# Where the left rows' layernorm sums are made and taken: two softmax stages, and a copy on ScalarE

## The chip, the cores and the metric

The kernel runs on one core of a Trainium2 chip. The metric is the device time of one execution in microseconds; of the kernel before there are three runs, and their median counts.

## The reference, cut to what matters

Rows are normalised (layernorm) and go through an attention layer that walks over 64 segments of 32 rows. Each segment puts 8 memory rows ahead of its 32 rows, attends over the 40, and hands on its first 8 output rows as memory to the next segment, so segments follow one another strictly. A small router part works on two chosen rows and is added at the end.

```
xn = layernorm(x)
for s in range(64):                       # segments of 32 rows
    h = concat([mem, xn[32*s:32*s+32]])   # 8 + 32 rows
    q, k, v = h @ Wq, h @ Wk, h @ Wv      # 32 heads of 128
    p = softmax(mask(q @ k.T * scale))
    o = (p @ v) @ Wo
    mem, out_s = o[:8], o[8:]
out = x + concat(out_s) + expert_of_two_rows(xn)
```

## The kernel before, in words

**Weights.** They are cut into 64 granules of 512 KB (48 for q, k and v, 16 for Wo). 44 stay in the SBUF; 20 are streamed again in each segment through 5 slots (`g`), one of them kept in PSUM instead. SP issues the fetches (L407); a fetch waits until TensorE has used up the granule that was in its slot.

**Order of a segment.** TensorE walks through phases 0 to 5 (q, k for heads 0 to 15, then q, k for heads 16 to 31, then v of both halves) with 8 granules each (`kc` 0 to 7), 4 matmuls a granule (L886), and then through the 16 granules of Wo (`w` 0 to 15, L615 and L619). Everything else hangs on these places by a table of hooks: `hook(p, kc, fn)` runs `fn` behind the matmuls of that granule, and hooks of one place run in the order in which they are entered. Since each engine works through its queue in order, the place of a hook is the place of its instructions in every queue that it uses.

**Attention in the hooks.** Each half of the heads goes through: transposes of q and k into the PSUM tile BT (L690), with copies out on ScalarE or VectorE (L698, L703, L705); scores into the PSUM tile BS (L713, L715) with mask and maximum on VectorE (L722 to L728); the exponent on ScalarE (L732); the rest of the softmax on VectorE (`soften`, L737 to L761); and `attend` on TensorE (L778, L780) with copies on ScalarE (L789, L791). The first half's scores are at (2,6), its exponent and softmax at (3,4), its `attend` at (5,4) and (5,6); the second half's transposes of k are at (4,3), its scores at (4,6), its exponent and softmax at (5,0), and its `attend` at w 5 and w 8. ScalarE copies the rows to be transposed (XB, L905) and the values (VM, L915) at each phase's end.

**Left rows.** A segment's last 8 rows ("left" rows) are not worked on in their own segment: those of four segments are gathered, 32 at a time, and go through the matmuls as extra passes over granules in the group before (L606, L639). Four segments make a group; the first segment of a group (`j == 0`) loads the next group's left rows and takes their layernorm statistics. That happens in the segments 4, 8, ..., 56; the preamble and segment 0 do it at once, by `stats_now`.

**Statistics.** `part_stats` (L206, L207) and `split_stats` (L210, L212, L213) are five small VectorE instructions in the tile SW; a row's elements lie in four groups of partitions, so `sum_stats` adds them up by small matmuls into BT's last columns (L216 for one order of rows, four times L219 for the other), and `take_sums` (L223) adds two halves and brings the sums back to SW, on VectorE. For the left rows `take_left` does that twice. In segments 4 to 56 these stood at (2,7), (4,0) and (4,1). `spread_of` (L227, L229) and `root_of` (L232, L233) make the factor of it, later. The next segment's own rows use the same S6, AV and HL columns of SW at (5,0).

BT carries the sums in columns 504 to 511, and the transposes and half of `attend` in others; what writes BT waits for those that read it before.

Of the kernel before, what the change touches and what calls it, by code (L numbers as in the profile page):

```python
# [51 lines left out]
def kernel(  # L52
# [16 lines left out]
    nc = tc.nc  # L69
# [9 lines left out]
    NT = S // P  # L79
# [79 lines left out]
    BT = psT.tile([P, 512], F32, name="BT")  # L159
# [6 lines left out]
    SW = const.tile([P, 24], F32, name="SW")  # L166
    S6, AV, HL, AB = SW[:, 0:6], SW[:, 6:8], SW[:, 0:2].bitcast(BF16), SW[:, 14:16]
    ROWS = [SW[:, 10:14], SW[:, 16:20]]
    NEGR, KMSK = SW[:, 20:21], SW[:, 21:22]
    OUTER = [SW[:, 8:10], SW[:, 22:24]]  # L170
    SPREAD, ROOT = SW[:, 2:3], SW[:, 3:4]
    SUMS = BT[:, 508:512]
    SUMS2 = BT[:, 504:508]
# [31 lines left out]
    def part_stats(x):  # L205
        nc.vector.bn_stats(out=S6, in_=x)  # L206
        nc.vector.bn_aggr(out=AV, in_=S6)  # L207

    def split_stats():
        nc.vector.scalar_tensor_tensor(out=AV[:, 1:2], in0=AV[:, 0:1], scalar=AV[:, 0:1], in1=AV[:, 1:2],  # L210
                                       op0=ALU.mult, op1=ALU.add)
        nc.vector.tensor_scalar(out=HL[:, 0:2], in0=AV, scalar1=0.25, scalar2=None, op0=ALU.mult)  # L212
        nc.vector.scalar_tensor_tensor(out=HL[:, 2:4], in0=AV, scalar=0.25, in1=HL[:, 0:2], op0=ALU.mult, op1=ALU.subtract)  # L213

    def sum_stats(crossed=False):
        nc.tensor.matmul(SUMS, lhsT=S4, rhs=HL, start=True, stop=True, skip_group_check=True)  # L216
        if crossed:
            for h in range(0, P, 32):
                nc.tensor.matmul(SUMS2[h:h + 32, :], lhsT=S1, rhs=HL, start=True, stop=True, tile_position=(0, h),  # L219
                                 skip_group_check=True)  # L220

    def take_sums(r, sums=SUMS):
        nc.vector.tensor_reduce(out=r[:, 0:2], in_=sums.rearrange("p (h c) -> p c h", h=2), axis=AX.X, op=ALU.add)  # L223

    def spread_of(r, to=None):
        to = r[:, 2:3] if to is None else to
        nc.vector.scalar_tensor_tensor(out=to, in0=r[:, 0:1], scalar=r[:, 0:1], in1=r[:, 1:2],  # L227
                                       op0=ALU.mult, op1=ALU.subtract)
        nc.vector.tensor_scalar(out=to, in0=to, scalar1=0.0, scalar2=1e-5, op0=ALU.min, op1=ALU.subtract)  # L229

    def root(of, to):
        nc.scalar.activation(out=to, in_=of, func=ACTF.Ln, scale=-1.0)  # L232
        nc.scalar.activation(out=to, in_=to, func=ACTF.Exp, scale=-0.5)  # L233

    def root_of(r):
        root(r[:, 2:3], r[:, 3:4])

    def take_left(G):
        take_sums(ROWS[1])
        take_sums(OUTER[G % 2], SUMS2)  # L240

    def stats_now(x, G=None):
        part_stats(x)
        split_stats()
        sum_stats(G is not None)
        if G is None:
            take_sums(ROWS[0])
        else:
            take_left(G)
        r = ROWS[G is not None]  # L250
        spread_of(r)
        root_of(r)
# [238 lines left out]
    todo_res = [g for g in resident if g not in res_tiles]  # L491

    stats_now(X[0][:, :])
    xn = norm_seg(0)
    stats_now(XL0, 0)
    norm_left(XL0)
    ST, STL = new_st(turn_rows(xn, XL0))
# [175 lines left out]
    for s in range(NSEG):  # L673
        G, j = divmod(s, 4)
# [6 lines left out]
        QT, KT, PTs, OT, nxt, sums = {}, {}, {}, {}, {}, {}  # L681
        hooks = {}

        def hook(p, kc, fn):
            hooks.setdefault((p, kc), []).append(fn)
# [21 lines left out]
        def scores(half):  # L707
            QKL = qkl[0]
            q, k = QT[half], KT[half]
            for il in range(4):  # L710
                for jq in range(4):
                    hh = 4 * il + jq
                    nc.tensor.matmul(SPS[32 * jq:32 * jq + 32, il, 0, :], lhsT=q[:, hh, :], rhs=k[:, hh, :],  # L713
                                     start=(il == 0), stop=True, tile_position=(0, 32 * jq), skip_group_check=True)
                    nc.tensor.matmul(SPS[32 * jq:32 * jq + XL, il, 1, :], lhsT=QKL[:, il, 2 * half, jq, :],  # L715
                                     rhs=k[:, hh, :], start=False, stop=True, tile_position=(0, 32 * jq),
                                     skip_group_check=True)
            for S4, m in ((SPS[:, :, 0, 0:XM], MASK), (SPS[:, :, 0, SEG:NK], None),
                          (SPS[:, :, 1, SEG:NK], MASK[:, 0:XL])):
                if m is not None:  # L720
                    m = m.unsqueeze(1).to_broadcast([P, 4, S4.shape[2]])
                    nc.vector.tensor_tensor(out=S4, in0=S4, in1=m, op=ALU.add)  # L722
                else:
                    nc.vector.tensor_scalar(out=S4, in0=S4, scalar1=NEGR, scalar2=None, op0=ALU.add)
            S8 = SPS.rearrange("p i a k -> p (i a) k")
            NM = one.tile([P, 8], F32, tag="nm", name="NM")
            nc.vector.tensor_reduce(out=NM[:, :], in_=S8, axis=AX.X, op=ALU.max, negate=True)
            nc.vector.tensor_tensor(out=S8, in0=S8, in1=NM[:, :].unsqueeze(2).to_broadcast([P, 8, NK]), op=ALU.add)  # L728
# [119 lines left out]
        if j == 0 and G + 1 < NT:  # L848
            hook(*((4, 1) if s == 0 else (1, 0)), get_left)
            if s > 0:  # L850
                hook(2, 7, lambda: part_stats(nxt["xl"]))
                hook(2, 7, split_stats)
                hook(4, 0, lambda: sum_stats(True))
                hook(4, 1, lambda: take_left(G + 1))
                hook(5, 7, lambda: spread_of(ROWS[1]))
            else:
                hook(5, 7, lambda: stats_now(nxt["xl"], G + 1))
# [5 lines left out]
            hook(2, 4, lambda: load_seg(s + 1))  # L863
        hook(4, 6, lambda: scores(1))
        hook(5, 0, exponent)
        if s + 1 < NSEG:
            hook(*((5, 0) if j == 0 else (4, 5)), lambda: part_stats(X[(s + 1) % 2][:, :]))
            hook(5, 0, split_stats)
        else:
            hook(1, 0, router_out)  # L870
            hook(1, 6, router_in)
# [232 lines left out]
```

## Time and profile before

| | |
|---|---|
| three runs | 1911.12, 1911.48, 1911.91 us |
| the profiled execution | 1903.86 us, its span 1902.2 us |
| mean TensorE clock | 0.954 |
| busy: PE, DVE, ACT, POOL | 84%, 52%, 41%, 24% of the span |
| TensorE idle at L690 until L223 | 30.5 us, 14 times |
| TensorE idle at L886 until a streamed granule | 59.8 us, 116 times |

The profile is of one execution. A timeline row gives the start, the busy time, the engine, the line, the operation with what it writes and reads, and in brackets how long the engine sat idle before it and who ended that. A row of waits gives the engine and line that waited, for whom, the total, how many times, and the longest. A window's row gives the busy time of each engine in it, then TensorE's granted clock (1.00 is full), the DMA engines' busy share and GB/s.

### The profile page before, as it was taken

To read this page: it belongs to the slowest core of one execution; us is meant where nothing else is said; L and a number is where in the kernel's file an instruction comes from. 1 tells how busy PE (TensorE), PEld (TensorE's weight loads), DVE (VectorE), ACT (ScalarE), POOL (GpSimd) and SP (SyncE) were. 2 spreads that over 40 slices of the span, in tenths; PEclk is the share of its full clock that TensorE was granted. 3 is DMA by queue.
4 is the path that set the end of the run, shared out by engine and by line. 5 is a ranking of instruction groups with operands and counts; after the bars stand their busy time and mean duration, and the time that the engine had idled before them with its cause. 6 is when DMAs were issued, how large, how long until landed. Compare 5 with 4: busy or idle time off the path is not lost.

```text
span 1902.2 us, 78103 instructions
## 1 busy us (share of the span) xinstructions
PE 1605.4 (84%) x33352; PEld 804.9 (42%) x33352; DVE 985.7 (52%) x3261; ACT 774.8 (41%) x2443; POOL 455.3 (24%) x895
## 2 busy tenths in 40 slices
PE   4478888988889989898888889898988989889864
PEld 2134444444444444444444444444444444444333
DVE  2135555555556555654565555556555555555540
ACT  1024444444444444444443444444444444444330
POOL 2212313222131313213131322323132221312120
PEclk9579999999999999999999999999999999999995
DMA  9999999999999999999999999999999999999998
GB/s 367 390 346 385 364 376 368 374 380 358 380 364 395 360 375 382 364 379 334 392 356 371 377 357 380 362 399 356 396 377 370 388 361 386 354 379 384 371 377 345
DMA packets 228061, 707.66 MB, mean 372 GB/s; under 512 B 38913, under 2 KB 52833, under 8 KB 227713
## 3 DMA queue, kind: packets, MB, share of 16 engines
q1 hardware_dynamic: 190272, 666.72, 92.4%
q0 software_dynamic: 28640, 28.03, 4.6%
q10 hardware_dynamic: 8800, 7.92, 1.2%
q8 instruction: 261, 4.28, 0.9%
q14 instruction: 88, 0.71, 0.1%
HBM read 689.86 MB, written 22.29 MB: 374 GB/s over the span
## 4 chain that ended last, share of the span: by engine, by line
DMA 56%; PE 37%; DVE 3%; ACT 2%; issue 1%; SPq 0%; POOL 0%; ACTq 0%; DVEq 0%; POOLq 0%
DMA g<-wsc 47%; PE PSm L886 21%; PE PSl L606 5%; PE BT L690 3%; PE WO L619 2%; PE WL L639 2%; DMA wres<-in_A_Wk_dram 2%; DMA wres<-in_A_Wv_dram 1%; DMA g<-in_A_Wo_dram 1%; DMA g<-in_A_Wv_dram 1%; DMA MW<-in_B_w_gate_dram 1%; DMA MW<-in_B_w_up_dram 1%; PE WO L615 1%; DMA X<-in_A_x_dram 1%; PE WO L778 1%
## 5 line engine op out<-in xcount | busy, mean ns | idle before, releaser
L886 PE MATMUL PSm<-wres,ST 128*32 128x512 bf16 x8448 | 709.3, 389 | 27.0 <-DMA wres<-in_A_Wv_dram 14.5
L886 PEld LDWEIGHTS <-ST 128*32 128x32 bf16 x12288 | 317.9, 97 | 390.8 <-issue 161.4
L886 PE MATMUL PSm<-g,ST 128*32 128x512 bf16 x3588 | 365.4, 393 | 70.7 <-DMA g<-wsc 59.8
L905 ACT CAST XB<-PSm 128x512 bf16<-128x512 f32 x256 | 150.6, 588 | 254.2 <-PE PSm L886 251.5
L522 POOL DMA_DIRECT2D LX<-ql_d x63 | 35.6, 564 | 653.1 <-PE WO L619 264.4
L705 DVE COPY KT<-BT 128x512 bf16<-128x512 bf16 x112 | 46.1, 411 | 280.7 <-PE BT L690 280.6
L972 POOL DMA_DIRECT2D out_dram<-X x256 | 129.4, 512 | 241.5 <-DVE X L970 219.5
L606 PE MATMUL PSl<-wres,STL 128*32 128x512 bf16 x2112 | 185.6, 392 | 0.2 <-ACT XBl L910 0.2
L318 POOL DMA_DIRECT2D X<-in_A_x_dram x252 | 127.3, 511 | 190.9 <-PE PSm L886 122.3
L430 ACT COPY BK<-KEPT 128x512 bf16<-128x512 bf16 x189 | 111.7, 605 | 136.9 <-DMA ql_d<-XBl 66.6
L619 PEld LDWEIGHTS <-OT 128*32 128x32 bf16 x4096 | 100.1, 96 | 107.2 <-issue 79.6
L619 PE MATMUL WO<-g,OT 128*32 128x256 bf16 x1536 | 78.0, 279 | 69.0 <-DMA g<-wsc 56.2
L690 PE MATMUL BT<-IDENT,XB 128*128 128x128 bf16 x1024 | 102.8, 224 | 32.2 <-DVE SW L223 30.5
L698 ACT COPY QT<-BT 128x512 bf16<-128x512 bf16 x128 | 74.9, 585 | 122.3 <-PE BT L529 73.5
L615 PE MATMUL WO<-wres,OT 128*32 128x512 bf16 x1536 | 122.2, 383 | 0.0
L690 PEld LDWEIGHTS <-XB 128*128 128x128 bf16 x1024 | 60.1, 98 | 139.4 <-ACT XB L905 69.1
L619 PE MATMUL WO<-wres,OT 128*32 128x256 bf16 x2560 | 115.4, 276 | 0.3 <-issue 0.3
L722 DVE TENSOR_TENSOR BS<-BS,CT 128x96 f32<-128x96 f32 (+1 forms) x256 | 59.4, 232 | 108.5 <-PE BS L715 103.7
L778 PEld LDWEIGHTS <-VM 32*128 32x128 bf16 x2048 | 65.3, 91 | 115.2 <-issue 88.6
L915 ACT CAST VM<-PSm 128x512 bf16<-128x512 f32 x128 | 75.9, 593 | 76.0 <-PE PSm L886 75.8
L606 PEld LDWEIGHTS <-STL 128*32 128x32 bf16 x3072 | 83.6, 98 | 50.1 <-issue 6.6
L703 ACT COPY KT<-QKL 128x128 bf16<-128x128 bf16 x128 | 38.1, 298 | 152.4 <-PE BT L690 152.4
(191 smaller groups left out, 2756.1 us busy)
## 6 DMA issues: line engine op xcount, KB each, us to landing
g<-wsc SPq DMA_DIRECT2D x1134, 512.0 KB, 6.2
g<-wsc SPq DMA_DIRECT2D x63, 256.0 KB, 5.7
LX<-ql_d POOLq DMA_DIRECT2D x63, 128.0 KB, 5.7
ql_d<-XBl ACTq DMA_DIRECT2D x60, 128.0 KB, 5.7
MW<-in_B_w_gate_dram SPq DMA_DIRECT2D x16, 448.0 KB, 9.5
MW<-in_B_w_up_dram SPq DMA_DIRECT2D x16, 448.0 KB, 9.0
wres<-in_A_Wk_dram SPq DMA_DIRECT2D x12, 512.0 KB, 15.9
wres<-in_A_Wq_dram SPq DMA_DIRECT2D x11, 512.0 KB, 5.3
```

What stands on the lines that cost most here:

```text
L318: by.dma_start(out=X[s % 2][32 * g:32 * g + XM, :], in_=x2[s * SEG:s * SEG + XM, 256 * block(g):256 * (block(g) + 1)])
L430: copy(out=back[c][:, :], in_=KEPT_COLS[KEPT_WHOLE][c])
L606: nc.tensor.matmul(PSl[32 * jq:32 * jq + 32, :], lhsT=STL[:, g % KC, :], rhs=part(Gv, jq), start=first_, stop=last_, tile_position=(0, 32 ...
L615: nc.tensor.matmul(PS[r0:r0 + 32, :], lhsT=lhs(h), rhs=Gv[:, D * hs + 512 * c:D * hs + 512 * (c + 1)], start=(w == 0), stop=(w == N_WIDE - ...
L619: nc.tensor.matmul(PS[32 * g:32 * g + 32, 0:256], lhsT=lhs(h), rhs=Gv[:, D * hs + 256 * block(g):D * hs + 256 * (block(g) + 1)], start=(w ...
L690: nc.tensor.transpose(out=PTq[:, il, :, :].rearrange("p j r -> p (j r)"), in_=XB[:, il * P:(il + 1) * P], identity=IDENT[:, :])
L698: nc.scalar.copy(out=QT[half][:, :, :], in_=pv)
L778: nc.tensor.matmul(o, lhsT=VM[half][q0:q0 + 32, il * P:(il + 1) * P], rhs=PTm[q0:q0 + 32, il, 0:NK], start=True, stop=False, tile_position ...
L886: nc.tensor.matmul(PSm[32 * jq:32 * jq + 32, :], lhsT=ST[:, 2 * block(kc // 2) + kc % 2, :], rhs=part(Gv, jq), start=(kc == 0), stop=(kc = ...
L905: nc.scalar.copy(out=XB[:, :], in_=PSm[:, :])
L915: nc.scalar.copy(out=VM[half][:, :], in_=PSm[:, :])
L972: nc.gpsimd.dma_start(out=out2[s * SEG:s * SEG + XM, 256 * block(g):256 * (block(g) + 1)], in_=OB[32 * g:32 * g + XM, :])
```

## The change

In segments 4, 8, ..., 56 the five statistics instructions of the left rows move from (2,7), behind the first half's scores, to (4,0), behind the first softmax. Their sums move from (4,0) to (4,7), behind the second half's scores. The sums are no longer taken out of BT by VectorE at (4,1): ScalarE copies all 8 columns to SW at (4,7) (`hold_left`), and VectorE adds the halves from there at (5,0), ahead of the next segment's statistics. `stats_now`, for the preamble and segment 0, gets the same copy.

```diff
+    def hold_left():
+        nc.scalar.copy(out=SW[:, 0:8], in_=BT[:, 504:512])
+
     def take_left(G):
-        take_sums(ROWS[1])
-        take_sums(OUTER[G % 2], SUMS2)
+        take_sums(ROWS[1], SW[:, 4:8])
+        take_sums(OUTER[G % 2], SW[:, 0:4])
...
         else:
+            hold_left()
             take_left(G)
...
             if s > 0:
-                hook(2, 7, lambda: part_stats(nxt["xl"]))
-                hook(2, 7, split_stats)
-                hook(4, 0, lambda: sum_stats(True))
-                hook(4, 1, lambda: take_left(G + 1))
+                hook(4, 0, lambda: part_stats(nxt["xl"]))
+                hook(4, 0, split_stats)
+                hook(4, 7, lambda: sum_stats(True))
+                hook(4, 7, hold_left)
...
         hook(5, 0, exponent)
+        if j == 0 and 0 < s and G + 1 < NT:
+            hook(5, 0, lambda: take_left(G + 1))
```

On VectorE, in segment 4, from the statistics of the left rows (BX) to the second half's scores (L722); L660 belongs to the left rows' output, L737 to L761 are the first softmax. Before:

```order
L206 BN_STATS SW<-BX 128x6
L207 BN_AGGR SW<-SW 128x2
L210 SCALAR_TENSOR_TENSOR SW<-SW 128x1
L212 TENSOR_SCALAR SW<-SW 128x2
L213 SCALAR_TENSOR_TENSOR SW<-SW 128x2
L660 TENSOR_TENSOR LF<-WL,LF 64x256 x2
L737 TENSOR_REDUCE DN<-BS 128x8
L738 RECIPROCAL DN<-DN 128x8
```

The softmax's other rows follow here, and behind its last (L761) stand the two L223 and then L722. After the change (lines are 4 higher there from `take_left` on) the same stretch ends so:

```order
L765 STREAM_TRANSPOSE PT_3655<-BX 128x256
L206 BN_STATS SW<-BX 128x6
L207 BN_AGGR SW<-SW 128x2
L210 SCALAR_TENSOR_TENSOR SW<-SW 128x1
L212 TENSOR_SCALAR SW<-SW 128x2
L213 SCALAR_TENSOR_TENSOR SW<-SW 128x2
L726 TENSOR_TENSOR BS<-BS,CT 128x4x24
L728 TENSOR_SCALAR BS<-BS,SW 128x4x8
L726 TENSOR_TENSOR BS<-BS,CT 128x4x8
L731 TENSOR_REDUCE NM<-BS 128x8
L732 TENSOR_TENSOR BS<-BS,NM 128x320
L223 TENSOR_REDUCE SW<-SW 128x2 x2
```

The five instructions moved from ahead of L660 and the softmax to behind it, and the two reductions from ahead of the second scores' five steps to behind them; they now read SW.

On TensorE, in segment 4 at (4,3), the last matmul of the granule and the first of the transposes into BT, with what each waits for. Before:

```order
L886 LDWEIGHTS ST
L886 MATMUL PSm<-wres_603,ST 32x512
L690 LDWEIGHTS XB [waits Activation_49]
L690 MATMUL BT<-IDENT,XB 128x128 [waits DVE_49]
L690 LDWEIGHTS XB
```

After:

```order
L892 LDWEIGHTS ST
L892 MATMUL PSm<-wres_604,ST 32x512
L694 LDWEIGHTS XB [waits Activation_49]
L694 MATMUL BT<-IDENT,XB 128x128
L694 LDWEIGHTS XB
```

The transposes no longer wait for VectorE; they still wait for ScalarE's copy of the rows.

On TensorE at (4,7), between the last granule of phase 4 (`g`) and the first of phase 5 (`wres_724`, in the changed kernel `wres_725`). Before:

```order
L886 LDWEIGHTS ST
L886 MATMUL PSm<-g,ST 32x512
L886 LDWEIGHTS ST
L886 MATMUL PSm<-wres_724,ST 32x512 [waits PE_49]
L886 LDWEIGHTS ST
```

After:

```order
L892 LDWEIGHTS ST
L892 MATMUL PSm<-g,ST 32x512
L216 LDWEIGHTS S_142
L216 MATMUL BT<-SW,S_142 128x4 [waits DVE_49]
L219 LDWEIGHTS S_147
L219 MATMUL BT<-SW,S_147 32x4
```

Three more pairs of L219 and then the granule `wres_725` follow. The sums, with their wait for VectorE's L213, now stand ahead of all of phase 5.

## The prediction

> **What bounds the kernel now.** First the page, for the span and for who is busy, then the same busy shares cut by segment: segment 4 (the first of a group, the only kind that the change touches) and segment 5 behind it.
>
> ```profile
> span 1902.2 us, 78103 instructions
> q1 hardware_dynamic: 190272, 666.72, 92.4%
> DMA 56%; PE 37%; DVE 3%; ACT 2%; issue 1%; SPq 0%; POOL 0%; ACTq 0%; DVEq 0%; POOLq 0%
> 204.80:233.20 28.40, 24.42 (x503) 12.10 (x496) 17.09 (x62) 13.03 (x43) 10.34 (x20) 0.94 0.97 352
> 233.20:260.10 26.90, 23.89 (x515) 12.11 (x511) 14.49 (x47) 11.55 (x36) 4.91 (x11) 1.00 1.02 389
> ```
>
> The last two rows give start:end, length, busy time of PE, PEld, DVE, ACT and POOL, then TensorE's clock, DMA share and GB/s. Weights stream all the time; where the slots are full, the stream waits for TensorE, and where they are empty TensorE waits for it. Segment 4 is 1.5 us longer than segment 5 although TensorE has no more instructions in it (503 against 515), and the stream moves 352 GB/s in it instead of 389. So something stops TensorE there, and the stream with it. The list of waits names it:
>
> ```profile
> PE PSm L886 <- DMA g<-wsc: 59.8, 116, 1.7
> PE BT L690 <- DVE SW L223: 30.5, 14, 2.5
> PE BT L216 <- DVE SW L213: 19.3, 16, 10.6
> ```
>
> The middle row has 14 waits, one in each first segment of a group from 4 to 56: 30.5 / 14 = 2.18 us each. In segment 4, TensorE's timeline and then VectorE's (start, us, what, and in brackets the idle time before it):
>
> ```profile
> 216.04 0.18 PE L216 MATMUL BT<-SW,S 128*128 128x4 bf16 x1 [0.36 <-DVE SW L213]
> 216.19 0.39 PE L886 MATMUL PSm<-g,ST 128*32 128x512 bf16 x4
> 219.17 0.38 PE L690 MATMUL BT<-IDENT,XB 128*128 128x128 bf16 x4 [2.16 <-DVE SW L223]
> 220.48 0.23 PE L713 MATMUL BS<-KT,QT 128*32 128x40 bf16 x4 [0.17 <-ACT KT L705]
> 221.12 1.10 PE L886 MATMUL PSm<-wres,ST 128*32 128x512 bf16 x8
> 223.44 0.21 PE L778 MATMUL WO<-PT,VM 32*128 32x40 bf16 x1
> 226.59 0.19 PE L778 MATMUL BS<-PT,VM 32*128 32x40 bf16 x1
> 231.38 0.40 PE L619 MATMUL WO<-g,OT 128*32 128x256 bf16 x8 [0.97 <-DMA g<-wsc]
> ```
> ```profile
> 214.70 0.42 DVE L206 BATCH_NORM_STATS2 SW<-BX 128x6 f32<-128x256 bf16 x1
> 215.82 0.16 DVE L213 SCALAR_TENSOR_TENSOR SW<-SW 128x2 bf16<-128x2 f32 x1
> 215.96 0.86 DVE L660 TENSOR_TENSOR LF<-WL,LF 64x256 f32<-64x256 f32 x2
> 217.96 0.29 DVE L756 TENSOR_TENSOR BX<-BS,DN 128x64 bf16<-128x64 f32 x1
> 218.56 0.45 DVE L761 STREAM_TRANSPOSE PT<-BX 128x256 bf16<-128x256 bf16 x1
> 218.93 0.19 DVE L223 TENSOR_REDUCE SW<-BT 128x2 f32<-128x4 f32 x2
> 221.00 0.27 DVE L722 TENSOR_TENSOR BS<-BS,CT 128x96 f32<-128x96 f32 x1 [1.89 <-PE BS L715]
> 225.67 0.45 DVE L761 STREAM_TRANSPOSE PT<-BX 128x256 bf16<-128x256 bf16 x1
> 226.04 0.12 DVE L223 TENSOR_REDUCE SW<-BT 128x2 f32<-128x4 f32 x1
> ```
>
> TensorE's sums (L216) were done at 216.3, but the two reductions that take them out of BT stand on VectorE behind L660 and the whole first softmax, until 219.12. The transposes (L690) write BT too, so they wait for them. The stop does two more things. Windows of the same segment, of the end of its stop and of segment 36:
>
> ```profile
> 216.90:220.30 3.40, 1.24 (x20) 0.63 (x17) 2.11 (x8) 0.66 (x2) 3.10 (x5) 1.00 0.98 376
> 220.30:223.70 3.40, 3.23 (x76) 1.44 (x71) 2.45 (x9) 1.14 (x3) 0.00 (x0) 0.50 0.79 231
> 220.20:228.20 8.00, 7.77 (x177) 3.67 (x176) 5.53 (x23) 4.05 (x20) 0.10 (x1) 0.79 0.84 272
> 228.20:233.20 5.00, 3.77 (x90) 2.19 (x81) 3.40 (x12) 2.76 (x10) 1.02 (x2) 1.00 1.03 404
> 1094.10:1097.50 3.40, 1.86 (x37) 0.65 (x26) 3.15 (x13) 2.01 (x5) 0.99 (x2) 1.00 1.03 401
> 1097.50:1100.90 3.40, 2.25 (x66) 1.38 (x69) 1.44 (x8) 1.16 (x3) 2.10 (x4) 1.00 0.78 252
> ```
>
> With TensorE busy for 1.24 of 3.40 us, the clock of the next 3.40 us is 0.50; with 1.86 busy (segment 36, where the stop falls across two windows) it stays 1.00. And with no slot freed, the stream drains: 272 GB/s for 8 us, against 404 after it, which is 8 x (404 - 272) / 404 = 2.6 us of streaming lost. The loss reaches the end by way of a fetch, as the chain of waits shows:
>
> ```profile
> 225.47 5.87 DMA g<-wsc
> ```
>
> This fetch is issued as the last granule of the attention phases is freed, takes 5.87 us, and ends the 0.97 us wait at 231.38.
>
> **The change, part by part**, for segment 4; the other 13 have the same wait.
>
> *The wait for L223 goes.* Removed are 0.36 us at L216 and 2.16 us at L690. What is late next for the transposes is ScalarE's copy of the rows that they turn:
>
> ```profile
> 215.19 0.74 ACT L657 COPY LF<-WL 64x256 f32<-64x256 f32 x2
> 216.28 0.59 ACT L905 CAST XB<-PSm 128x512 bf16<-128x512 f32 x1
> L791 ACT CAST OTL<-BT 128x32 bf16<-128x32 f32 x256 | 56.0, 219 | 0.0
> ```
>
> It ends at 216.87, so L690 starts at 216.95 instead of 219.17. The second scores follow 220.48 - 219.17 = 1.31 us later, at 218.26, and they must not overwrite BS before the softmax has read it, at 217.96 + 0.29 = 218.25: no more than 0.05 us of waiting, 218.3.
>
> *A wait at the sums comes.* Five statistics instructions ran from 214.70 to 215.98, 1.28 us, while VectorE would have waited anyway for ScalarE's L657 (done at 215.93). Now they run behind the softmax: 218.56 + 0.45 = 219.01, plus 1.28, is 220.29. TensorE is at the sums at 218.3 + (221.12 - 220.48) = 218.94, waits 1.35 us, spends 216.19 - 216.04 = 0.15 us on them and goes on at 220.45, not at 221.12. That is a gain of 0.67 us; everything of TensorE stands behind this wait, the next granules and their slots with it.
>
> *The clock.* The longest idle time left is 1.35 us, so a window keeps 3.40 - 1.35 = 2.05 us of work, less some short bits, and 1.86 kept the clock. I take it as full. The stretch from 221.12 to the first attention at 223.44, 2.32 us at half clock, then takes 1.16, and that attention comes at 221.6, 1.8 us earlier. The page "TensorE: Matmul & The Clock Gate" of the Trainium skill, section "Part 1: The HAM clock gate", has the clock fall only after an idle window of about 3.4 us. By that rule a stop of 2.16 us costs no clock and its removal returns none: the 1.16 us would not come, and the sum would be the first rival's, 14 us. The two windows above disagree with it, since part of a window was enough, and I go by them.
>
> *ScalarE's copy of the sums* (hold_left) is 128x8 out of BT; the nearest row is L791, 219 ns. It runs from 220.45 to about 220.75 where ScalarE is idle. The copy of the values behind it (0.59 us, as L905) ends at 221.35, before the attention at 221.6. If that cover goes, it costs some tenths.
>
> *VectorE's chain.* The second scores' steps start at 220.25 instead of 221.00, 0.75 us earlier, but the reductions of the held sums now stand in the chain: 0.19 us as the old pair took, at most 0.24, twice the single row's 0.12. So the chain to the second softmax's end moves 0.56 us: from 226.12 to 225.56, with the last L223 at 225.6. TensorE would be at the second half's attention 3.15 us (226.59 - 223.44) after 221.6, at 224.75, and waits for VectorE until 225.6. Here the gain is 226.59 - 225.6 = 1.0 us.
>
> *The stream.* Slots are freed sooner: the fetch at 225.47 would be issued some 1.8 us earlier and land as much earlier if nothing is in its way. TensorE reaches it at 231.38 - 0.97 - 1.0 = 229.4, so at most the whole wait of 0.97 goes too. The stream is busier then and part of the lost 2.6 us stays lost in the new 1.35 us stop; I take half, 0.5 us.
>
> *The rest.* No DMA is moved, none of SP or POOL. The preamble and segment 0 get the copy between sums and reductions too, 0.22 us each as L791, at most twice that with the handover; both lie in the start, where the first weights are still being loaded, and I put them at nothing.
>
> Sum: 14 x (1.0 + 0.5) = 21 us. The profiled execution took 1903.86 us, with a span of 1902.2, 7.6 us below the median of 1911.48, so it would become 1882.9. The median, less the same 21, is 1890.5. The ends: 14 x 0.67 us with half of that given back to the stream is 5 us, 1906; the whole stop gone, 14 x 2.52 us, is 35 us, 1876.
>
> **The rivals.**
>
> *The clock still falls.* The 0.05 us at the scores, 1.35 at the sums and short idle bits lie close together; a window placed badly could keep less than 1.86 us of work. Then TensorE gains only the 0.67 us, arrives at the second attention at 225.9, behind VectorE, and with a third of a microsecond from the stream it is 1.0 us in each segment: 14 us, 1897.5. By the Trainium skill's rule above, 1.35 us would not cause it.
>
> *The whole stop counts.* If the waits for weights shrink with the full clock by as much as the stream lost, 2.5 us come back in each: 1876. For it speaks 272 against 404 GB/s; against it the new wait at the sums.
>
> *The stream takes it all.* DMA is busy for 0.97 of segment 4, and segment 36, with its clock kept, waited longer for weights instead. Then TensorE only waits elsewhere: 1911. Against it speaks the 0.84 share over 8 us.
>
> *The new wait is longer than the old: slower.* It decides at the moment when L213 ends. At 220.96 (0.67 later than worked out) nothing is gained, and if the statistics, now on the way from first softmax to second scores, ended at 221.5, then TensorE, the scores' steps and the second softmax would all be 0.5 us later than before: 14 x 0.5 = 7 us, 1918.5. For it speaks that they had a free place before and have none now; against it, that VectorE has nothing else to do in between, and five such instructions have taken 1.28 us.
>
> **How the numbers follow.** Forecast 0.55; clock still falls 0.16; whole stop 0.10; the stream takes it 0.12; slower 0.07. About 0.2%, 3.8 us, is what a measurement here can tell from no change, so faster is 0.55 + 0.16 + 0.10 = 0.81, same 0.12, slower 0.07. The predicted time is the forecast's 1890.5. The range from 1876 to 1906 leaves out the last two and is set by the ends above.
>
> **What would show it.** The row of 14 waits for L223 at L690 should be gone, and in its place 14 waits of TensorE at L216 for L213 with about 1.35 us each; short waits of L690 for ScalarE's XB; some waits at the second attention for VectorE; a clock of 1.00 behind most of the stops and a mean clock above 0.954; first segments of a group about 1.5 us shorter and above 352 GB/s. I am wrong if waits for L213 are above 2 us, if the clock falls as often, or if the first segments shorten while the waits for weights grow by the same.

## The result, and the profile after

The changed kernel took 1881.25 us (median of 4 runs, 1874.42 to 1886.88) against 1911.3 us for the kernel before (4 runs beside it, 1908.26 to 1911.91). The ratio is 0.9844 [0.9808, 0.9880], so 30 us less, 23 to 37 by the interval. A second comparison, run with the last experiments, gave 1882.31 against 1907.66: 0.9872 [0.9824, 0.9921], 25 us. The forecast was 1890.5 with a range from 1876 to 1906. The profiled execution took 1883.29 us instead of 1903.86, 20.6 less, where the sum had said 21.

The mean TensorE clock rose from 0.954 to 0.963. The page of the changed kernel:

```profile
span 1881.6 us, 78147 instructions
q1 hardware_dynamic: 190272, 666.72, 93.1%
```

TensorE's waits: first a row of before that the prediction does not show (the waits of Wo's granules for weights; those at PSm, L886, were 59.8 us, 116 times), then the rows of the changed kernel. From `take_left` on its lines are 4 to 6 higher: L694 is L690 of before, L892 is L886, L623 is L619, L784 the second line of the attention.

```profile
PE WO L619 <- DMA g<-wsc: 56.2, 82, 1.7
```
```profile
PE PSm L892 <- DMA g<-wsc: 59.3, 119, 1.6
PE WO L623 <- DMA g<-wsc: 40.9, 70, 1.9
PE BT L216 <- DVE SW L213: 34.4, 30, 10.8
PE BT L694 <- ACT XB L911: 6.8, 13, 0.6
PE BS L784 <- DVE SW L223: 4.2, 14, 0.3
PE WO L782 <- ACT OTL L795: 3.6, 14, 0.3
```

The row of 14 waits for L223 at the transposes is gone. The new wait for L213 at the sums is there: 30 times in place of 16, 15.1 us more in all. Of the 30, 14 are the new stop at (4,7), 1.26 us each in the mean, and 14 are short ones of 0.18 us at the next segment's own sums, whose statistics now stand on VectorE behind the two reductions. The other two lie ahead of segment 4, as before. Three more small waits have come up: 0.5 us each for ScalarE's XB, 0.3 us each for VectorE at the second half's attention, and 0.26 us each for ScalarE's OTL inside the first half's (2 of them before, 1.1 us). The waits for weights at WO are 56.2 - 40.9 = 15.3 us shorter, those at PSm as long as before.

The windows of the changed kernel: segments 4 and 5, then the 8 us behind the new stop, then the two stretches of 3.4 us of which the first holds that stop.

```profile
204.80:232.20 27.40, 23.70 (x504) 12.04 (x496) 17.12 (x62) 13.30 (x44) 10.34 (x20) 1.00 1.02 385
232.20:259.00 26.80, 23.88 (x515) 12.28 (x511) 14.49 (x47) 11.66 (x36) 4.98 (x11) 1.00 1.02 386
221.10:229.10 8.00, 7.03 (x160) 3.69 (x159) 6.62 (x28) 5.01 (x25) 0.67 (x2) 1.00 1.01 370
218.40:221.80 3.40, 1.89 (x65) 0.87 (x61) 3.10 (x13) 1.02 (x4) 2.50 (x5) 1.00 1.02 402
221.80:225.20 3.40, 2.90 (x73) 1.47 (x65) 3.06 (x12) 2.21 (x11) 0.00 (x0) 1.00 1.04 380
```

Segment 4 is 28.40 - 27.40 = 1.0 us shorter and moves 385 GB/s where it moved 352. The stretch with the stop has 1.89 us of work and the next one keeps the clock at 1.00, where before it fell to 0.50; the stream moves 370 GB/s in the 8 us behind it, not 272.

Segment 4 on TensorE and VectorE in the changed kernel. Everything comes 0.90 us later here than in the trace of before, even ahead of the change, so 0.90 has to be taken off before a time is held against the prediction's. Both segments start at 204.8, so from there on segment 4 gains 1.0 + 0.9 = 1.9 us.

```profile
217.81 0.40 PE L694 MATMUL BT<-IDENT,XB 128*128 128x128 bf16 x4 [0.46 <-ACT XB L911]
219.19 0.21 PE L717 MATMUL BS<-KT,QT 128*32 128x40 bf16 x4 [0.23 <-DVE BX L760]
219.41 0.43 PE L892 MATMUL PSm<-g,ST 128*32 128x512 bf16 x4
221.12 0.16 PE L216 MATMUL BT<-SW,S 128*128 128x4 bf16 x1 [1.29 <-DVE SW L213]
221.26 0.60 PE L892 MATMUL PSm<-wres,ST 128*32 128x512 bf16 x8
222.44 0.19 PE L782 MATMUL WO<-PT,VM 32*128 32x40 bf16 x1
224.40 0.16 PE L216 MATMUL BT<-SW,S 128*128 128x4 bf16 x1 [0.18 <-DVE SW L213]
226.46 0.17 PE L784 MATMUL BS<-PT,VL 32*128 32x40 bf16 x1 [0.31 <-DVE SW L223]
226.50 0.17 PE L782 MATMUL BT<-PT,VM 32*128 32x40 bf16 x1
230.12 0.39 PE L623 MATMUL WO<-g,OT 128*32 128x256 bf16 x8
```
```profile
219.44 0.45 DVE L765 STREAM_TRANSPOSE PT<-BX 128x256 bf16<-128x256 bf16 x1
219.81 0.39 DVE L206 BATCH_NORM_STATS2 SW<-BX 128x6 f32<-128x256 bf16 x1
220.91 0.16 DVE L213 SCALAR_TENSOR_TENSOR SW<-SW 128x2 bf16<-128x2 f32 x1
222.74 0.21 DVE L223 TENSOR_REDUCE SW<-SW 128x2 f32<-128x4 f32 x2
225.96 0.45 DVE L765 STREAM_TRANSPOSE PT<-BX 128x256 bf16<-128x256 bf16 x1
```

The five statistics now fill VectorE from 219.81 to 221.07, between the first softmax and the second scores, and TensorE waits 1.29 us for the last of them. The last row on TensorE has no wait in front: the granule that came 0.97 us late before lies ready now.

To see where the time came from in the whole program, all 14 first segments (4, 8, ..., 56) were added up, before and then changed:

```profile
sum 413.50, PE 343.92 PEld 172.25 DVE 239.01 ACT 182.51 POOL 145.23; mean PE 24.57 PEld 12.30 DVE 17.07 ACT 13.04 POOL 10.37
```
```profile
sum 382.40, PE 329.07 PEld 166.59 DVE 239.41 ACT 185.50 POOL 144.75; mean PE 23.50 PEld 11.90 DVE 17.10 ACT 13.25 POOL 10.34
```

That is 29.5 us each before and 27.3 now, 31.1 us less together. Of these, 343.92 - 329.07 = 14.9 us are busy time that TensorE needs less for the same matmuls, at the higher clock; the rest is idle time. The 14 segments of one execution scatter by 0.5 to 1.3 us, so a mean of 14, here and below, is good to some 0.1 to 0.4 us. The next windows run from segment 4 to the end of segment 59, and from there to the end: before, the changed kernel, and its second profiled execution.

```profile
204.80:1736.50 1531.70, 1362.54 (x28637) 683.02 (x28630) 850.11 (x2815) 672.43 (x2128) 381.96 (x743) 0.98 1.00 372
1736.50:1902.20 165.70, 110.98 (x2442) 59.63 (x2434) 66.97 (x210) 49.24 (x151) 30.93 (x60) 0.83 0.96 368
```
```profile
204.80:1712.20 1507.40, 1349.03 (x28638) 677.95 (x28630) 849.42 (x2815) 676.67 (x2142) 382.75 (x743) 1.00 1.01 379
1712.20:1881.60 169.40, 113.36 (x2439) 61.27 (x2434) 67.05 (x209) 49.20 (x151) 30.96 (x60) 0.81 0.96 362
```
```profile
201.80:1711.80 1510.00, 1351.52 (x28638) 679.62 (x28630) 850.62 (x2816) 675.52 (x2142) 381.96 (x743) 1.00 1.01 378
1711.80:1877.60 165.80, 110.41 (x2439) 60.10 (x2434) 66.70 (x209) 49.47 (x151) 30.90 (x60) 0.83 0.97 368
```

Segments 4 to 59 are 24.3 us shorter in the one execution and 21.7 in the other. Of the 31.1 us of the first segments, 31.1 - 24.3 = 6.8 us were given back in the other 42 segments of that execution. The last stretch was 3.7 us longer in one execution and the same (165.8) in the other, so that loss belongs to the execution and not to the change.

### The profile page after: what moved, and what is told of

The parts are those of the page before. It is cut to its first block, busy times and chain, and to the rows that moved or that the text cites. A ratio compares the mean times of both kernels' runs of the same rounds, so it can differ in the third digit from the quotient of the medians.

```text
span 1881.6 us, 78147 instructions
## 1 busy us (share of the span) xinstructions
PE 1595.7 (85%) x33352; PEld 802.1 (43%) x33352; DVE 985.0 (52%) x3261; ACT 779.6 (41%) x2459; POOL 456.2 (24%) x895
## 5 line engine op out<-in xcount | busy, mean ns | idle before, releaser
L892 PE MATMUL PSm<-wres,ST 128*32 128x512 bf16 x8448 | 698.4, 383 | 25.6 <-DMA wres<-in_A_Wv_dram 15.7
L892 PEld LDWEIGHTS <-ST 128*32 128x32 bf16 x12288 | 316.1, 96 | 390.5 <-issue 154.8
L892 PE MATMUL PSm<-g,ST 128*32 128x512 bf16 x3588 | 359.6, 387 | 72.1 <-DMA g<-wsc 59.3
L623 PEld LDWEIGHTS <-OT 128*32 128x32 bf16 x4096 | 99.5, 96 | 89.6 <-issue 65.2
L619 PE MATMUL WO<-wres,OT 128*32 128x512 bf16 x1536 | 123.7, 387 | 1.0 <-issue 0.8
L623 PE MATMUL WO<-g,OT 128*32 128x256 bf16 x1536 | 77.8, 278 | 52.8 <-DMA g<-wsc 40.9
L623 PE MATMUL WO<-wres,OT 128*32 128x256 bf16 x2560 | 115.2, 276 | 0.4 <-issue 0.4
L694 PE MATMUL BT<-IDENT,XB 128*128 128x128 bf16 x1024 | 102.1, 222 | 8.4 <-ACT XB L911 6.8
L694 PEld LDWEIGHTS <-XB 128*128 128x128 bf16 x1024 | 58.6, 98 | 117.5 <-ACT XB L911 75.9
L438 DVE COPY g<-KEPT 128x512 bf16<-128x512 bf16 x126 | 47.6, 420 | 87.6 <-PE PSm L892 34.2
```

Source lines behind the costliest of these rows:

```text
L619: nc.tensor.matmul(PS[r0:r0 + 32, :], lhsT=lhs(h), rhs=Gv[:, D * hs + 512 * c:D * hs + 512 * (c + 1)], start=(w == 0), stop=(w == N_WIDE - ...
L623: nc.tensor.matmul(PS[32 * g:32 * g + 32, 0:256], lhsT=lhs(h), rhs=Gv[:, D * hs + 256 * block(g):D * hs + 256 * (block(g) + 1)], start=(w ...
L694: nc.tensor.transpose(out=PTq[:, il, :, :].rearrange("p j r -> p (j r)"), in_=XB[:, il * P:(il + 1) * P], identity=IDENT[:, :])
L892: nc.tensor.matmul(PSm[32 * jq:32 * jq + 32, :], lhsT=ST[:, 2 * block(kc // 2) + kc % 2, :], rhs=part(Gv, jq), start=(kc == 0), stop=(kc = ...
```

## The experiments

The theory, once the result was seen: the stop of TensorE costs by the fetches that it holds up, so what matters is how much idle time is left at the stop, and the first microsecond or so at the new place is covered by weights that lie in their slots. Rivals: it costs by the halved clock behind it; and the place of the stop matters beside its length. Beside that, which of the three parts of the change is needed. Each kernel was compared with the kernel before on its chip, whose median there was 1906.6 to 1907.7 us. The medians below are of 4 to 10 runs. Executions of one program differed more on these chips than in the first comparison (the kernel before from 1888 to 1922), so ratios and the lengths of the first segments carry the verdicts.

**early_stats**: the changed kernel, but the statistics stay where they were, behind the first half's scores. Sums, copy and adding are late.

```diff
-                hook(4, 0, lambda: part_stats(nxt["xl"]))
-                hook(4, 0, split_stats)
+                hook(2, 7, lambda: part_stats(nxt["xl"]))
+                hook(2, 7, split_stats)
```

> The changed kernel, but with the left rows' five statistics instructions back at (2,7), ahead of the first softmax; sums, ScalarE's copy and reductions stay where the change put them. Theory (a stop of TensorE starves the stream of weights, and the stream is what sets a first segment's time): the wait at L216 for L213 (1.29 to 1.46 us in the changed kernel) is gone in segments 4 to 56 and VectorE's chain starts 1.3 us earlier, but a first segment of a group takes 27.3 us and the others 26.7 to 26.9, so only some 0.4 us are left to gain: 14 x 0.4 = 6 us, about 1875. Rival (each us of stop counts in full): 14 x 1.35 = 19 us, about 1862.

Measured: 1874.72 us, 0.9837 [0.9781, 0.9893]. Its 14 first segments, and two rows of its waits:

```profile
sum 383.10, PE 333.15 PEld 168.01 DVE 238.79 ACT 186.07 POOL 144.79; mean PE 23.80 PEld 12.00 DVE 17.06 ACT 13.29 POOL 10.34
```
```profile
PE PSm L892 <- DMA g<-wsc: 73.3, 144, 1.8
PE BT L216 <- DVE SW L213: 16.0, 12, 10.8
```

No stop at the sums is left (16.0 us, less than the 19.3 of before), and yet the first segments are 27.4 us long, as with the change. TensorE waits for weights instead: 73.3 us at PSm where it was 59.3. In these segments the stop that the change brought cost nothing that can be seen; early_stats_5, below, leaves a doubt.

**hold_early**: ScalarE's copy alone. Statistics and sums stay at their old places; the copy to SW stands right behind the sums, and VectorE adds the halves later. Against the changed kernel:

```diff
-                hook(4, 0, lambda: part_stats(nxt["xl"]))
-                hook(4, 0, split_stats)
-                hook(4, 7, lambda: sum_stats(True))
-                hook(4, 7, hold_left)
+                hook(2, 7, lambda: part_stats(nxt["xl"]))
+                hook(2, 7, split_stats)
+                hook(4, 0, lambda: sum_stats(True))
+                hook(4, 0, hold_left)
```

> The kernel before with one part of the change: ScalarE copies the sums out of BT at (4,0), right behind the sums, and VectorE adds the halves from the copy at (5,0); statistics stay at (2,7), sums at (4,0). The transposes at (4,3) then wait only for ScalarE (XB's copy and then the 0.2 us copy, about 217.1 in the before's segment 4, against 219.17). Theory: with the stop gone and no new one, the same as early_stats within 4 us, about 1875, which would show that the move of statistics and sums did nothing for the gain and cost a little. Rival (the move of the statistics is what helps): as the kernel before, above 1900.

Measured: 1881.01 us, 0.9887 [0.981, 0.9964]; first segments:

```profile
sum 379.00, PE 332.44 PEld 167.18 DVE 239.35 ACT 185.83 POOL 144.73; mean PE 23.75 PEld 11.94 DVE 17.10 ACT 13.27 POOL 10.34
```

379.00 / 14 = 27.1 us. The copy alone does all that the change does; moving the statistics and the sums added nothing that these runs can tell. It was expected within 4 us of early_stats and came 6 us above it, with an interval 29 us wide.

**stats_twice** and **stats_thrice**: the changed kernel with the first two statistics instructions (L206, L207) run two and three times (the result is the same), so that the stop at the sums grows at its new place.

```diff
                 hook(4, 0, lambda: part_stats(nxt["xl"]))
+                hook(4, 0, lambda: part_stats(nxt["xl"]))
                 hook(4, 0, split_stats)
```

That is stats_twice; stats_thrice has the added line two times.

> The changed kernel with the first two statistics instructions (L206, L207) made twice at (4,0), so that the sums wait 0.65 us longer: some 1.95 to 2.1 us at L216 instead of 1.29 to 1.46. Theory of the stream: 14 x 0.65 = 9 us slower than the changed kernel, about 1890, whether or not the clock falls. Rival (the clock is what cost time in the kernel before): if the clock stays full, within 4 us of the changed kernel; if it falls to 0.50 behind most of the stops, 14 x 1.2 = 16 us more, about 1905.

> The changed kernel with L206 and L207 made three times at (4,0): the stop at L216 grows to about 2.65 us (1.44 in the changed kernel, 2.03 with them made twice). Theory (only the length beyond some 1.4 us counts): first segments go from 28.4 us with the stop of 2.03 to 29.4, as in the kernel before with its 2.24 + 0.38 us; ratio to the kernel before 0.998 to 1.002. Rival (the place counts, a stop at (4,7) costs less than one at (4,3)): 28.8 us or less, ratio 0.994 or less.

Measured: 1895.31 us, 0.993 [0.9901, 0.9958], and 1908.36 us, 1.0006 [0.9964, 1.0047]. First segments and the wait at the sums, first of stats_twice, then of stats_thrice (a row of the windows and a row of the waits each):

```profile
sum 397.40, PE 339.10 PEld 166.99 DVE 247.87 ACT 184.57 POOL 144.83; mean PE 24.22 PEld 11.93 DVE 17.71 ACT 13.18 POOL 10.34
```
```profile
PE BT L216 <- DVE SW L213: 42.3, 21, 10.8
```
```profile
sum 406.80, PE 341.23 PEld 166.80 DVE 256.09 ACT 184.68 POOL 145.22; mean PE 24.37 PEld 11.91 DVE 18.29 ACT 13.19 POOL 10.37
```
```profile
PE BT L216 <- DVE SW L213: 50.7, 20, 10.8
```

Taken segment by segment, the idle time at L213 is 1.44 us in the mean of the changed kernel's first segments, 2.03 and 2.62 here; the stop at (4,7) alone, without the short wait at the next segment's sums, is 1.26, 1.95 and 2.55 us. The segments are 27.3, 28.4 and 29.1 us long. So up to 1.26 us the stop shows no cost in them (27.4 without it, 27.3 with it), and from there to 2.55 each microsecond costs (29.1 - 27.3) / (2.55 - 1.26) = 1.4 us.

Not all of that is the stream's. The clock fell in 9 of the 14 first segments of stats_twice and in 10 of stats_thrice, and in none of the changed kernel's. Those that kept it at 1.00 are 27.9 us long (5 of stats_twice) and 28.7 us (4 of stats_thrice), the others 28.7 and 29.2. At full clock a microsecond of stop then costs some (28.7 - 27.3) / (2.55 - 1.26) = 1.1 us, an estimate from few segments, and the rest goes with the clock. So stats_twice lies between its theory (1890, whatever the clock does) and its rival (1905 with the clock halved behind most stops), and the cost of the stream and that of the clock stay mixed in it.

By the time of the whole program the gain of the change is gone at 2.55 us; by its segments four fifths of it is. The slower rival of the prediction, a longer wait at L213, is thus real as a mechanism, but it set the point too early: it had nothing left of the gain when L213 ends 0.67 us later, and stats_twice, 0.69 us later, still gains 0.7%.

**busy_stop**: the kernel before, with 24 matmuls whose result nobody uses put into its stop, in the 14 segments concerned.

```diff
+        def keep_busy(t):
+            for n in range(6):
+                for jq in range(4):
+                    nc.tensor.matmul(t[32 * jq:32 * jq + 32, :], lhsT=ST[:, 0, :], rhs=part(res_tiles[35], jq),
+                                     start=True, stop=True, tile_position=(0, 32 * jq))
...
+                if p == 3 and j == 0 and s > 0 and G + 1 < NT:
+                    hooks[p + 1, 3].insert(0, lambda t=PSm: keep_busy(t))
```

> The kernel before with 24 matmuls put ahead of the transposes at (4,3) in segments 4 to 56, into the accumulator that ScalarE has already copied, so that TensorE works through some 1.3 us of the 2.16 us stop; they compute nothing that is used. The stop's end is not moved. Theory of the stream: the clock stays full (mean clock about 0.963 instead of 0.954) and the time does not change by more than 4 us, 1907 to 1915. Rival (the halved clock behind the stop is a good part of what the change took back): 12 x 1.16 = 14 us faster, about 1897.

Measured: 1897.74 us, 0.9957 [0.9925, 0.9988]. The clock, a wait, and the first segments:

```profile
core 0: 1909.1 us, clock 0.965
```
```profile
PE BT L690 <- DVE SW L223: 11.3, 14, 1.1
```
```profile
sum 415.10, PE 350.98 PEld 180.06 DVE 239.21 ACT 182.15 POOL 145.05; mean PE 25.07 PEld 12.86 DVE 17.09 ACT 13.01 POOL 10.36
```

The mean clock is as high as the changed kernel's (0.965 against 0.963), but the first segments are 29.65 us long, as in the kernel before. The profiled execution was the slowest of its ten, 13 us above their median, so the segments may be somewhat long; the times give 2 to 14 us for the clock out of the 23 to 37. The kernel before points the same way: two of its first segments, 36 and 48, kept the clock at 1.00, and they are no shorter than the mean of 29.5.

```profile
1083.20:1113.50 30.30, 23.41 (x504) 12.17 (x496) 17.13 (x63) 13.06 (x43) 10.38 (x20) 1.00 0.97 357
1407.80:1437.30 29.50, 23.34 (x500) 12.08 (x496) 17.04 (x62) 13.06 (x43) 10.31 (x20) 1.00 0.98 355
```

So the clock was the smaller part, and how small stays open within that interval.

**mid_take**: the kernel before, with the first softmax's last transposes put behind the two reductions, so that L223 ends earlier and the old stop is shorter, at its old place.

```diff
+            def turn_it():
...
+            if half == 0 and j == 0 and s > 0 and G + 1 < NT:
+                hook(4, 1, turn_it)
+            else:
+                turn_it()
```

> The kernel before, with VectorE's two reductions (L223) put ahead of the first softmax's two last instructions (its transposes) in segments 4 to 56: nothing else moves, ScalarE copies nothing. They end about 0.8 us sooner, so the stop at L690 is 1.3 to 1.5 us instead of 2.16, at its old place. Theory (the first 1.4 us or so of a stop are covered by weights that lie in the slots, only what is beyond starves the stream): a first segment of a group falls from 29.5 us to about 27.5, as in the changed kernel; 14 x 2 = 28 us less, ratio 0.985. Rival (the place counts: a stop at (4,3) keeps slots that a stop at (4,7) does not): 0.8 us less in each at most, 28.7 us, ratio 0.994.

Measured: 1895.1 us, 0.9936 [0.9906, 0.9966].

```profile
sum 402.90, PE 336.55 PEld 171.16 DVE 239.71 ACT 182.63 POOL 146.37; mean PE 24.04 PEld 12.23 DVE 17.12 ACT 13.05 POOL 10.45
```
```profile
PE BT L690 <- DVE SW L223: 19.1, 14, 1.7
```

Here `turn_it` holds the transposes that close the softmax. The stop at TensorE's transposes is 19.1 / 14 = 1.4 us, nearly as short as the changed kernel's 1.26 at the sums, but the first segments are 28.8 us, not 27.3. So length alone doesn't set the price; the place does too. The 0.38 us at the sums, which this kernel keeps, make it 1.8 us of stop, and 28.8 us is what some 2 to 2.5 us cost at the new place (28.4 and 29.1 above). The clock fell in 7 of the 14 here, but the 7 that kept it are 28.4 us long, still above 27.3. With longer stops the place shows less: stats_thrice, with 2.62 us of idle time at L213, is 29.1 us, and the kernel before, with 2.18 + 0.38 us at the old place, 29.5, so there the theory of the length (29.4) came nearer than its rival (28.8 or less).

**take_on_vector**: the changed kernel without ScalarE's copy: sums late, and VectorE takes them out of BT at (5,0).

```diff
+    def take_bt(G):
+        take_sums(ROWS[1])
+        take_sums(OUTER[G % 2], SUMS2)
...
-                hook(4, 7, hold_left)
...
-            hook(5, 0, lambda: take_left(G + 1))
+            hook(5, 0, lambda: take_bt(G + 1))
```

> The changed kernel without ScalarE's copy in segments 4 to 56: VectorE takes the sums out of BT itself, at the place where it adds the copied halves in the changed kernel, behind the second scores' steps; statistics and sums stay where the change put them. The first attention (L778 in the kernel before) then waits for it, since it writes BT: until about 1.4 us behind the end of the stop at L216, where TensorE would be after 1.2 us, so 0.3 to 0.6 us more. Theory (stops that short are covered): the changed kernel's time within 4 us, first segments 27.3 to 27.6 us, ratio 0.984 to 0.986. Rival (the copy is what makes the gain): first segments above 28.5 us, ratio above 0.994.

Measured: 1884.33 us, 0.9888 [0.9806, 0.9971].

```profile
sum 383.30, PE 332.77 PEld 165.99 DVE 237.92 ACT 183.01 POOL 144.62; mean PE 23.77 PEld 11.86 DVE 16.99 ACT 13.07 POOL 10.33
```

27.4 us again, as the theory had it; the ratio came out above its 0.984 to 0.986, which the interval holds. With late sums the copy isn't needed; with the copy (hold_early) late sums aren't. Either part ends the wait of the transposes behind VectorE's queue, and as far as these runs can tell that is the whole of the change's worth.

**slot_ahead**: the kernel before, with granule 35 in a streamed slot in place of 36, so that a slot is freed just ahead of the old stop. It asks if the place matters through the slot that was freed last.

```diff
-STREAMED = [2, 5, 6, 9, 13, 17, 21, 25, 29, 33, 36, 39, 42, 45, 47, 50, 53, 56, 59, 62]
+STREAMED = [2, 5, 6, 9, 13, 17, 21, 25, 29, 33, 35, 39, 42, 45, 47, 50, 53, 56, 59, 62]
...
-    "v0": {(2, 7, 0): [32, 34, 35], (2, 8, 0): [37, 38], (3, 4, 1): [33], (3, 4, 4): [36], (3, 4, 7): [39]},
+    "v0": {(2, 7, 0): [32, 34, 36], (2, 8, 0): [37, 38], (3, 4, 1): [33], (3, 4, 3): [35], (3, 4, 7): [39]},
```

> The kernel before, streaming granule 35 of phase 4 instead of granule 36 (which stays in the SBUF instead), with its extra pass moved along: the stop at (4,3) keeps its length and place, but a slot is now freed right ahead of it and the next one only at (4,7), as it is around the stop at (4,7) in the changed kernel. Theory (a slot freed just ahead of a stop gives the stream work for it, and so the stop at (4,7) is cheap): first segments fall from 29.5 to 28.5 us or less, ratio 0.993 or less. Rival (the longest time without a fetch is what counts, and that grows from 3.4 to about 4.1 us here): 29.5 us or more, ratio 1.000 or more.

Measured: 1910.99 us, 1.0024 [0.9993, 1.0054].

```profile
sum 405.60, PE 344.79 PEld 172.84 DVE 239.06 ACT 182.40 POOL 145.81; mean PE 24.63 PEld 12.35 DVE 17.08 ACT 13.03 POOL 10.41
```
```profile
PE BT L690 <- DVE SW L223: 26.2, 14, 2.2
```

The first segments came out at 29.0 us, 0.5 shorter, which is hardly more than their scatter, and no time was gained. The stop did not keep its length, either: it is 26.2 / 14 = 1.9 us, not 2.2. The result lies between the theory (28.5 or less) and the rival (29.5 or more), so the experiment didn't settle it: why a stop at the transposes costs more than one at the sums stays open.

**hold_mid**: as hold_early, with sums and copy at (4,2). **early_stats_5**: early_stats again, in more runs. **after_again**: the changed kernel, beside them on the same chip.

> hold_early with the sums and ScalarE's copy at (4,2) instead of (4,0), so that neither the sums wait for L213 (0.43 us in each first segment there) nor the transposes for VectorE. Theory (such short stops are covered): within 3 us of hold_early and early_stats, ratio to the kernel before 0.981 to 0.987. Rival (every us counts): 14 x 0.4 = 6 us below hold_early.

> early_stats once more, beside hold_mid and the changed kernel on one chip. Theory: no difference beyond 0.3% among the three, ratio to the kernel before 0.981 to 0.987. Rival (the stop of 1.44 us that the change left still costs): 0.5% or more below the changed kernel.

> The changed kernel itself, in the same rounds as the two above. Theory: ratio to the kernel before 0.984 to 0.989, since the profiles put the gain at 1.74 us in each of 14 groups, 24 us, and some of it may be lost in the last segments. Rival (the first comparison's 30 us hold): 0.984 or less.

Measured: hold_mid 1879.49 us, 0.9835 [0.9784, 0.9885]; early_stats_5 1870.35 us, 0.9822 [0.9778, 0.9867]; after_again 1882.31 us, 0.9872 [0.9824, 0.9921]. The first segments of hold_mid are the shortest of all, 374.90 / 14 = 26.8 us:

```profile
sum 374.90, PE 328.38 PEld 167.51 DVE 238.98 ACT 185.53 POOL 145.10; mean PE 23.46 PEld 11.97 DVE 17.07 ACT 13.25 POOL 10.36
```

early_stats was the faster by its median in both comparisons (0.9837 and 0.9822 against 0.9844 and 0.9872). In the second, with six runs each in the same rounds, it was 12 us, 0.6%, faster than the changed kernel; that is what the rival of early_stats_5 asked for (0.5% or more) and more than the theory allowed (0.3%). It was also 9 us faster than hold_mid, where 3 us had been expected. Segments 4 to 59 of its profiled execution took 1495.6 us, 14.4 less than after_again's 1510.0:

```profile
207.20:1702.80 1495.60, 1347.19 (x28638) 677.60 (x28630) 849.57 (x2815) 676.44 (x2142) 381.95 (x743) 1.00 1.01 381
```

In the first pair of profiles these segments took 1507.4 us in both, and the intervals of the ratios overlap. So it isn't shown that early_stats beats the changed kernel, nor that the stop which the change left is free.

Last, where the time of the first segments lies, in us for one segment, rounded: TensorE's busy time (from the rows above), its idle time that the landing of weights ended, and its other idle time.

| kernel | length | busy | waits for weights | other waits |
|---|---|---|---|---|
| before | 29.5 | 24.6 | 2.0 | 3.0 |
| changed | 27.3 | 23.5 | 0.8 | 3.0 |
| early_stats | 27.4 | 23.8 | 2.4 | 1.1 |
| hold_early | 27.1 | 23.7 | 2.5 | 0.9 |
| mid_take | 28.8 | 24.0 | 2.3 | 2.4 |
| stats_thrice | 29.1 | 24.4 | 0.9 | 3.8 |

The change did not make TensorE wait less for other engines: 3.0 us before and after. It put the waits where the stream lost less by them and the clock didn't fall, and what shrank are the waits for weights and the busy time. Where nearly all of the other waits are gone (early_stats, hold_early), waits for weights take their place and the length stays near 27.

## Why the prediction was right

*The wait for L223 goes.* The transposes start at 217.81 - 0.90 = 216.91 (predicted 216.95) and wait for ScalarE's copy of XB, as said. The wait at the scores for the softmax was 0.23 us, not 0.05.

*A wait at the sums comes.* L213 ends at 221.07 - 0.90 = 220.17 (220.29); the sums run at 220.22 and TensorE goes on at 220.36 (220.45). The stop is 1.29 us here and 1.26 in the mean (1.35). The prediction did not have the 0.18 us at the next segment's sums.

*The clock.* It stayed at 1.00 in all 14 first segments, where it had fallen in 12 of 14, and the first attention comes at 221.54 (221.6). The Trainium skill's page "TensorE: Matmul & The Clock Gate", section "Part 1: The HAM clock gate", has the clock fall after an idle window of about 3.4 us. These traces disagree, as the prediction had it: part of a window was enough (1.24 us of work in 3.40 us, and 0.50 behind it). But the gain that the prediction took from the clock came out right for the whole path, not for the clock's own share; busy_stop gives that only 2 to 14 us, and early_stats shows that what the path gains above the stream's pace is lost in waits for weights.

*ScalarE's copy.* It took 0.17 us (219 ns assumed), and the values that it copies behind that were ready in time for the first attention. The waits of 0.26 us for OTL, 14 of them, the prediction did not have; they lie inside the first attention, ahead of the second, which waits for VectorE anyway.

*VectorE's chain.* The second softmax ends at 226.41 - 0.90 = 225.51 (225.56) and the attention is at 226.50 - 0.90 = 225.6 (225.6), 1.0 us sooner than before, with 14 waits of 0.3 us for VectorE, of the kind foretold. By the sum they would have been 225.6 - 224.75 = 0.85 us; the small waits ahead of them, for OTL and at the next segment's sums, took the rest.

*The stream.* This was the term that was mis-sized the most. It was put at 0.5 us; in segment 4 the whole wait of 0.97 us went, and over all first segments 31.1 / 14 = 2.2 us were gained instead of 1.5, of which 0.5 was given back in the segments behind them. The prediction had nothing of that loss. With 370 GB/s in the 8 us behind the stop, not 272, the stream lost little in the new stop, and to count half of the old loss as still lost was too careful. Net it is 24.3 / 14 = 1.7 us in one profiled execution and 21.7 / 14 = 1.55 in the other, for a sum of 1.5. That the net came so near is in part luck: the stream gave more than was put down, and the segments behind took some of it back.

The median moved by 30 and 25 us in the two comparisons, where the two profiled executions were 21 and 25 us shorter; the sum of 21 lies just below the first interval (23 to 37) and inside the second (15 to 34). The measured 1881.25 us is thus nearer to the rival in which the whole stop counts (1876) than to the forecast (1890.5), and so are the first segments by themselves (2.2 us gained, for 2.5 and 1.5); the second comparison's 25 us are nearer to the forecast's 21 than to that rival's 35. That a measurement here can tell 0.2% from no change was too hopeful: the intervals are 0.3 to 0.8% wide on each side.

Two things were right by the prediction's sum but not by its picture. It gave all three parts of the change a role, and either the copy or the late sums would have done. And it priced each microsecond of TensorE's path alike; the runs show first segments in which a stop of 1.26 us at (4,7) has no visible cost and each microsecond above it costs 1.4 us, the clock's part included.

## What to carry to other kernels

In a kernel that is fed by a stream, a stop of TensorE costs through the slots that it doesn't free in time: compare the GB/s of the microseconds behind a stop with those of an undisturbed stretch before pricing the stop by its length. A stop may cost little up to some length and more than its own length above it, so a change that leaves one just below that point should be tried with the stop a little longer. Where an engine waits to write into a bank that another has to read out first, look at what stands ahead of that read in its queue; an idle engine can copy the few columns out in 0.17 us.

## What the runs showed of the hardware

The clock fell when about half of a 3.4 us stretch was idle: 1.24 us of work in 3.40 gave 0.50 in the next, 1.86 and 1.89 us left it at 1.00. In the records of these traces the granted clock changes on a grid of 3.413 us. Cut on that grid (from 140 to 1700 us, all 13 traces, stretches at full clock), 43 of the 45 stretches with under 1.6 us of TensorE work were followed by 0.50, 16 of the 35 with 1.6 to 1.8 us, and 23 of the 5771 with more. A kernel that kept the clock at 0.965 by matmuls nobody needs got its first segments no shorter in its one trace (29.65 against 29.5 us), and at most 14 us in all. Over segments 4 to 59 of the changed kernel the DMA engines of the one core moved 379 GB/s in the mean. And the same program, run again on one chip, differed by up to 1.4% (1895 to 1922 us in 19 runs), more than most of these experiments are apart.
